# Top-k attention with a dropless mixture of experts: tails of the transposed weights in the score banks

## The chip, the cores and the metric

One core of one Trainium2 chip. The metric is the device time of one launch in microseconds (us); 1531.04 us is the median of three runs of the kernel before (1531.03 to 1531.17). Engines: TensorE (PE, with its weight loads as PEld), VectorE (DVE), ScalarE (ACT), GpSimd (POOL), and SyncE (SP), which issues most transfers.

## The reference

```python
# q, k, v: (8, 8, 576, 64) float32
scores = (q @ k.T) / 8                          # per batch and head, 576 x 576
kth    = 32nd largest score of each row
attn   = softmax over the scores >= kth         # the rest weighs nothing
x      = (attn @ v) laid out as (4608, 512)
# experts: 8, w1 (512, 1024), w2 (1024, 512) each
logits = x @ w_gate
e      = argmax(logits);  gate = softmax(logits)[e]
y      = gate * (relu(x @ w1[e]) @ w2[e])       # each token in its own expert alone
```

## The kernel before

**Units and iterations.** A unit is one batch and two heads; there are 32, four to a batch. A unit's score rows are nine tiles of 128 rows (four per head, and one that holds the last 64 rows of both heads). They are worked in five groups: `groups` 0 to 3 are pairs (the same rows of both heads), group 4 is the single ninth tile. `loop()` runs over all 160 groups; one turn of it is an iteration.

**One iteration i**, in the order in which `loop()` writes it (inside `tc.manual_schedule`, so TensorE, ScalarE and VectorE keep exactly this order; GpSimd's elementwise steps are kept in order too):

1. VectorE: `fold` and `search`. `fold` takes maxima and minima of the two halves of a score row, `fold_on` halves the maxima once more and puts them into the tile `few` (L262), with the few largest of what was put aside. `search` finds the 32nd largest by four rounds of eight maxima (L307) and three replacements into `scr` (L314). `fold_on` of the next group is called inside this search, before its last round.
2. ScalarE: the small `low` (L323), then `depths`: one Relu per tile (L337), which marks scores below the threshold.
3. GpSimd: `less`, a subtraction per tile (L346), then `doubts` (L327), which reads `few`.
4. ScalarE: `scores(i + 3)`, copies of the score products of three iterations ahead from PSUM into `s` (L245).
5. `transposed(i - 1)`: TensorE turns the weights of the group before. Four 128x128 transposes per tile (L371) go into a bank `wTm` and are copied by ScalarE into `wT` (L374, L376). The last 64 columns of each tile, the tails (L380), go into a bank `wTl` of their own and are copied into `wTt` (L383, L385). `bank()` hands out the two banks of the pool `ps_t` in turn, for these and for everything else of attention.
6. ScalarE: `weights`, one Exp per tile (L357).
7. TensorE: `products(i + 4)`, the score products (L236) into PSUM tiles `sc` of two banks each, two tiles in the pool `ps_s`.
8. In certain iterations, steps of the unit's ending: in group 3, and again in the next unit's group 0, half of the outputs `po` (L401) with ScalarE's copy into `oT` (L403); in group 1 transposes back (`px`, `pl`) and the gate's logits, with copies (L418 to L420). Once a batch, ranks (L476 to L482) in group 4 and the copy of `run` (L800). `ending()` is a generator; `at_place()` moves it on at named places.

**Expert blocks.** A block is 128 tokens of one expert: `xtp` transposes, 32 products `ph` in eight pieces of four (each half of `ph` ends in a Relu copy `hT`, L651), eight pieces `py` (L661), and a scaled copy `y` (L675) that GpSimd then stores. `pieces(n)` runs the next n pieces of the current block on TensorE, and ends early where the block pauses (before `py`, so that `hT` can be made) or where the next block's rows aren't on chip yet; the rest goes back into `credit`. Copies that a piece makes due wait in the list `due` until `evacuate()` writes them into ScalarE's order. Pieces come in two calls per iteration: half of `now` between the transposes and the tails, the rest at the iteration's end. Expert rows are known once a batch has been routed, so pieces begin after about 400 us. After the last unit, the remaining blocks run alone.

**Buffers in play.** [...] `few` has two buffers, `scr` two, `s` four, `w` three.

Of the kernel before, what the change touches and what calls it, by code (L numbers as in the profile page):

```python
# [9 lines left out]
F32 = mybir.dt.float32  # L10
# [25 lines left out]
def kernel(  # L36
# [39 lines left out]
    nc = tc.nc  # L76
    B, U, P, _, S = qk.shape
# [3 lines left out]
    D = P // 2  # L81
# [119 lines left out]
    def bank(name):  # L201
        return k.ps_t.tile([P, SM], F32, name=name, tag="t")
# [23 lines left out]
    def products(n, tiles):  # L226
        todo = []
        got = []
        for i in tiles:
            ps = k.ps_s.tile([P, 2, SM], F32, name="sc")  # L230
            todo += [(ps, h, rows, cols) for h, rows, cols in parts(i)]
            got.append(ps)
        for j in range(2):
            for ps, h, rows, cols in todo:
                d = slice(h * D, (h + 1) * D)
                nc.tensor.matmul(  # L236
                    ps[rows, j, 0:HF], n.q[d, cols], n.k[d, j * HF:(j + 1) * HF], start=True, stop=True
                )
        return got

    def scores(got):

        s = k.att.tile([P, 2, 2, HF], F32, name="s", bufs=2 if k.exact else 4)
        return s, [
            lambda m=m, ps=ps: nc.scalar.copy(s[:, m, :, :], ps[:, :, 0:HF]) for m, ps in enumerate(got)  # L245
        ]

    def fold(tiles, s):

# [8 lines left out]
    def fold_on(tiles, f):  # L258

        m2 = slice(0, len(tiles))  # L260
        f.few = k.att.tile([P, 2, LW], F32, name="few")
        nc.vector.tensor_tensor(f.few[:, m2, 0:QF], f.h[:, m2, 0:QF], f.h[:, m2, QF:HF], op=ALU.max)  # L262
        f.hl = k.att.tile([P, 2, QF], F32, name="hl", bufs=1)
        nc.vector.tensor_tensor(f.hl[:, m2, :], f.h[:, m2, 0:QF], f.h[:, m2, QF:HF], op=ALU.min)
# [16 lines left out]
    def search(n, tiles, s, f, then=lambda: None):  # L281

        m_all = range(len(tiles))
        m2 = slice(0, len(tiles))
        tops = k.small.tile([P, 2, TOP_K], F32, name="tops", bufs=4)
        if k.exact:
            src = [s[:, m, :, :].rearrange("p j k -> p (j k)") for m in m_all]
            width = S
        else:
            src = [f.few[:, m, :] for m in m_all]  # L290
            width = LW
            for m in m_all:
                for j, away in enumerate((f.l[:, m, :], f.hl[:, m, 0:QF // 2], f.hl[:, m, QF // 2:QF])):
                    nc.vector.max(out=f.few[:, m, QF + 8 * j:QF + 8 * j + 8], in_=away)  # L294
        scr = k.att.tile([P, 2, width], F32, name="scr")
        nbias = k.small.tile([P, 2], F32, name="nbias", bufs=3)
        R = TOP_K // 8

        def quiet(r):

            return r >= (1 if len(tiles) == 2 else 2)

        for r in range(R):
            if r == R - 1:
                then()
            for m in m_all:
                nc.vector.max(out=tops[:, m, r * 8:(r + 1) * 8], in_=src[m])  # L307
# [15 lines left out]
        nc.scalar.activation(low[:, m2], thr[:, m2], AF.Copy, scale=STEEP)  # L323

        def doubts():
            c = 2 * tiles[0] if len(tiles) == 2 else 2 * NC
            k.last_pool = in_turn(nc.gpsimd.tensor_tensor(  # L327
                n.over[:, c:c + len(tiles), :], f.few[:, m2, QF + 7:LW:8], _inner(thr[:, m2], NL), op=ALU.subtract
            )).ins

        return low, nbias, doubts
# [27 lines left out]
                    accum_out=n.z[:, c + m:c + m + 1],  # L359
                )  # L360

    def transposed(n, tiles, w):

        pair = len(tiles) == 2
        if tiles[0] == 0:
            n.wT = k.wtp.tile([P, NC, 2, S], F32, name="wT")
            n.wTt = k.wtp.tile([ST, 2, S], F32, name="wTt")
        for m, i in enumerate(tiles):
            pm = bank("wTm")
            for c in range(NC):  # L370
                nc.tensor.transpose(pm[:, c * P:(c + 1) * P], w[:, m, c * P:(c + 1) * P], ident)  # L371
            pm4 = pm[:, :].rearrange("p (c q) -> p c q", c=NC)
            if pair:
                nc.scalar.copy(n.wT[:, :, m, tiles[0] * P:(tiles[0] + 1) * P], pm4)  # L374
            else:
                nc.scalar.copy(n.wT[:, :, :, SM:S], pm4.rearrange("p c (h q) -> p c h q", h=2))  # L376
        yield
        pt = bank("wTl")
        for m in range(len(tiles)):
            nc.tensor.transpose(pt[0:ST, m * P:(m + 1) * P], w[:, m, SM:S], ident)  # L380
        if pair:
            q = slice(tiles[0] * P, (tiles[0] + 1) * P)
            nc.scalar.copy(n.wTt[:, :, q], pt[0:ST, 0:2 * P].rearrange("p (h q) -> p h q", h=2))  # L383
        else:
            nc.scalar.copy(n.wTt[:, :, SM:S], pt[0:ST, 0:P].rearrange("p (h q) -> p h q", h=2))  # L385

    def outputs(n, x):

# [303 lines left out]
    with ExitStack() as st:  # L692
# [147 lines left out]

        got_of, s_of, f_of, w_of = {}, {}, {}, {}

        def turning(i):
            b, u, g = work[i]
            return transposed(unit[b * U + u], g, w_of.pop(i))

        def multiply(i):
            b, u, g = work[i]
            got_of[i] = products(unit[b * U + u], g)
            if g == groups[-1] and b * U + u + 2 < len(units):  # L850
                unit.append(load_unit(*units[b * U + u + 2]))

        def loop():
            nonlocal credit, rate, clock
            for i in range(min(AHEAD, len(work))):
                multiply(i)
                s_of[i], steps = scores(got_of.pop(i))
                for step in steps:
                    step()
            multiply(AHEAD)  # L860
            f_of[0] = fold(work[0][2], s_of[0])
            fold_on(work[0][2], f_of[0])
            for i, (b, u, g) in enumerate(work):
# [28 lines left out]
                credit -= now  # L892
                clock = i
                if i + AHEAD < len(work):
                    s_of[i + AHEAD], steps = scores(got_of.pop(i + AHEAD))
# [20 lines left out]
            for _ in turning(len(work) - 1):  # L916
                pass
            assert len(late) == 1
            clock = None
            for count, _ in enumerate(late[0][0]):  # L920
# [24 lines left out]
    with ExitStack() as outer:  # L945
# [10 lines left out]
        with ExitStack() as st:  # L956
# [7 lines left out]
            with tc.For_i(0, B, 1) as b:  # L964
# [3 lines left out]
                for u in range(U):  # L968
# [1 line left out]
                    load_values(n)  # L970
                    open_unit(n)
                    for g in groups:
                        s, steps = scores(products(n, g))
# [6 lines left out]
                        for _ in transposed(n, g, w):  # L980
                            pass
                    for _ in outputs(n, x):
                        pass
                    for _ in divisors(n):
# [67 lines left out]
```

## Time and profile before

| | |
|---|---|
| median of three runs | 1531.04 us |
| the profiled execution | 1531.07 us, its span 1529.5 us |
| TensorE busy | 1334.9 us (87%), granted clock 0.91 on average |
| VectorE busy | 1134.8 us (74%) |
| ScalarE busy | 944.1 us (62%) |
| GpSimd busy | 646.5 us (42%) |
| DMA, mean | 151 GB/s |

By stages: from 0 to 400 us TensorE is busy 295.5, VectorE 371.2, ScalarE 276.5 us; from 400 to 1235 us 786.8, 756.2 and 622.6 us; from 1235 us on TensorE 252.6 of 294 us, and VectorE next to nothing.

In the rows of the profile `L371` is line 371 of the kernel; `wTm<-ident,w` says that an instruction writes `wTm` from `ident` and `w`. A time in brackets behind a row is how long its engine had stood idle, and who ended it. A matmul of this kernel is recorded twice, so a pair's eight transposes and its eight records of four score products are what their rows count.

### The profile page before, as it was taken

The page shows a single profiled execution, that of the slowest core. Times are in us where ns is not written, and L with a number is a line of the kernel's source. Part 1 is how long each engine was busy: PE and PEld are TensorE (multiplying, and loading weights), DVE is VectorE, ACT ScalarE, POOL GpSimd, SP SyncE. Part 2 cuts the span into 40 slices and gives each one's busy share as a digit, 9 for nine tenths or more (in the row PEclk, how much of TensorE's full clock was granted, in tenths as well). Part 3 has the DMA queues.
Part 4 walks back from the last instruction along what each step waited for, and adds up shares of the span by engine and source line. Part 5 has one row for each costly group of instructions (what it writes and reads, how often), then busy time and mean ns, then how long its engine had stood idle before and what let it go on. Part 6 is the DMA issues. An engine that isn't in the chain of part 4 may idle for free. (4 is left out here: it accounts for less than half of the span.)

```text
span 1529.5 us, 25597 instructions
## 1 busy us (share of the span) xinstructions
PE 1334.9 (87%) x8034; PEld 889.8 (58%) x8034; DVE 1134.8 (74%) x4702; ACT 944.1 (62%) x2097; POOL 646.5 (42%) x837
## 2 busy tenths in 40 slices
PE   5777777788799989998999999989999994999996
PEld 3444444445466656666666666657666672677673
DVE  7999989998999999999789989997899820000000
ACT  4777767765777778786776777777767640111110
POOL 3445456444644555464444644554436431000000
PEclk9877868765899999999999999999999996999998
DMA  2000011001534363526444444454444458688883
GB/s 71 25 25 25 25 38 43 25 25 37 197 135 168 126 219 129 183 96 244 171 158 163 173 149 151 154 175 176 170 173 173 164 182 270 248 293 317 302 305 133
DMA packets 101937, 230.70 MB, mean 151 GB/s; under 512 B 5150, under 2 KB 25630, under 8 KB 101792
## 3 DMA queue, kind: packets, MB, share of 16 engines
q1 hardware_dynamic: 95328, 209.00, 38.6%
q0 software_dynamic: 6464, 19.97, 3.6%
q8 instruction: 66, 1.08, 0.3%
q14 instruction: 79, 0.65, 0.1%
HBM read 207.68 MB, written 22.33 MB: 150 GB/s over the span
## 5 line engine op out<-in xcount | busy, mean ns | idle before, releaser
L346 POOL TENSOR_TENSOR w<-s,w 128x576 f32<-128x576 f32 x288 | 402.7, 1417 | 588.6 <-ACT w L337 588.5
L646 PEld LDWEIGHTS ph<-xTs,w 128*128 128x128 f32 x2560 | 301.2, 193 | 29.3 <-issue 29.3
L646 PE MATMUL ph<-xTs,w 128*128 128x128 f32 x2560 | 317.5, 279 | 0.0
L661 PE MATMUL py<-w,hT 128*128 128x512 f32 x640 | 296.8, 607 | 1.8 <-ACT hT L651 1.8
L236 PE MATMUL sc<-qkb 64*128 64x288 f32 (+1 forms) x1280 | 237.8, 495 | 23.9 <-ACT s L245 17.1
L307 DVE MAX8 tops<-scr 128x8 f32<-128x168 f32 x864 | 253.7, 323 | 2.3
L357 ACT ACTIVATE w<-w,nbias 128x576 f32<-128x576 f32 x288 | 221.4, 771 | 0.9 <-POOL w L346 0.9
L337 ACT ACTIVATE w<-s,low 128x576 f32<-128x576 f32 x288 | 209.5, 769 | 5.2
L661 PEld LDWEIGHTS py<-w,hT 128*128 128x128 f32 x640 | 117.2, 193 | 122.9 <-issue 118.1
L371 PE MATMUL wTm<-ident,w 128*128 128x128 f32 x1152 | 180.1, 300 | 9.2 <-ACT x L419 8.1
L371 PEld LDWEIGHTS wTm<-ident,w 128*128 128x128 f32 x1152 | 143.2, 153 | 62.5 <-issue 26.4
L314 DVE MATCH_REPLACE8 scr<-tops,scr 128x168 f32<-128x168 f32 x576 | 179.3, 317 | 0.0
L236 PEld LDWEIGHTS sc<-qkb 64*128 64x128 f32 (+1 forms) x1280 | 121.4, 203 | 92.0 <-issue 33.2
L245 ACT COPY s<-sc 128x576 f32<-128x576 f32 x288 | 168.3, 628 | 9.7 <-PE sc L236 9.7
L380 PE MATMUL wTl<-ident,w 128*64 128x128 f32 x288 | 65.7, 304 | 113.6 <-ACT wT L374 112.8
L401 PE MATMUL po<-wT,vb 128*64 128x288 f32 x1024 | 162.3, 467 | 0.6 <-ACT wT L376 0.6
L374 ACT COPY wT<-wTm 128x512 f32<-128x512 f32 x256 | 138.2, 597 | 26.2 <-PE wTm L371 26.0
L667 POOL DMA_INDIRECT out_dram<-y,xg x40 | 44.2, 1106 | 230.8 <-ACT y L675 226.8
L262 DVE TENSOR_TENSOR few<-h 128x288 f32<-128x288 f32 (+1 forms) x160 | 75.0, 469 | 75.7 <-POOL doubt L327 75.1
L294 DVE MAX8 few<-l 128x8 f32<-128x288 f32 x288 | 129.0, 448 | 0.0
L401 PEld LDWEIGHTS po<-wT,vb 128*64 128x64 f32 x1024 | 77.3, 157 | 84.1 <-issue 36.9
L253 DVE TENSOR_TENSOR h<-s 128x576 f32<-128x576 f32 (+1 forms) x160 | 116.2, 726 | 5.6 <-ACT s L245 5.6
(125 smaller groups left out, 1478.4 us busy)
## 6 DMA issues: line engine op xcount, KB each, us to landing
w<-in_moe_w_dram SPq DMA_DIRECT2D x80, 2048.0 KB, 12.8
qkb<-in_qk_dram SPq DMA_DIRECT2D x32, 576.0 KB, 4.1
xg<-x_rows SPq DMA_DIRECT2D x40, 257.0 KB, 2.7
vb<-in_v_dram SPq DMA_DIRECT2D x32, 320.0 KB, 3.2
x_rows<-blank SPq DMA_DIRECT2D x5, 257.0 KB, 10.0
x_rows<-blank POOLq DMA_DIRECT2D x4, 257.0 KB, 8.1
x_rows<-x,posi POOLq DMA_INDIRECT x40, 3.3
out_dram<-y,xg POOLq DMA_INDIRECT x40, 3.3
```

What stands on the lines that cost most here:

```text
L236: nc.tensor.matmul(ps[rows, j, 0:HF], n.q[d, cols], n.k[d, j * HF:(j + 1) * HF], start=True, stop=True)
L245: lambda m=m, ps=ps: nc.scalar.copy(s[:, m, :, :], ps[:, :, 0:HF]) for m, ps in enumerate(got)
L307: nc.vector.max(out=tops[:, m, r * 8:(r + 1) * 8], in_=src[m])
L314: nc.vector.match_replace(out=scr[:, m, :], in_to_replace=tops[:, m, r * 8:(r + 1) * 8], in_values=src[m], imm_value=NEG,)
L337: nc.scalar.activation(w[:, m, :], s[:, m, :, :].rearrange("p j k -> p (j k)"), AF.Relu, scale=-STEEP, bias=low[:, m:m + 1],)
L346: k.last_pool = in_turn(nc.gpsimd.tensor_tensor(w[:, m, :], s[:, m, :, :].rearrange("p j k -> p (j k)"), w[:, m, :], op=ALU.subtract)).ins
L357: nc.scalar.activation(w[:, m, :], w[:, m, :], AF.Exp, scale=scale, bias=nbias[:, m:m + 1], accum_out=n.z[:, c + m:c + m + 1],)
L371: nc.tensor.transpose(pm[:, c * P:(c + 1) * P], w[:, m, c * P:(c + 1) * P], ident)
L374: nc.scalar.copy(n.wT[:, :, m, tiles[0] * P:(tiles[0] + 1) * P], pm4)
L401: nc.tensor.matmul(po[r, 0:HF], lhsT, rhs, start=(c == 0), stop=(c == KC - 1))
L646: nc.tensor.matmul(ph[:, f, :], n.w1[:, 0, dt, fc * P:(fc + 1) * P], n.xT[:, dt, :], start=(dt == 0), stop=(dt == DT - 1),)
L661: nc.tensor.matmul(py, hT[:, f, :], n.w2[:, 0, f, :], start=(f == 0), stop=(f == FT - 1))
```

## The change

The score banks become one tile of four banks, `score_room()`, one buffer for a whole group. A score row uses 288 of the 512 columns of each bank; the transposed tails go into columns 288 to 415 of the same tile. So the iteration takes its room first, the tails are turned into it right behind the other transposes, and the score products of that iteration go into it afterwards. All copies of the turn then follow on ScalarE in one stretch: both of `wT`, then one of `wTt`.

`few` gets three buffers, `scr` one. `evacuate()` moves from behind the Relu marks to behind the score copies. In iterations with outputs, back transposes or ranks, and in every group 3, all pieces come behind those (`first` is 0); elsewhere the first half comes between tails and products. A block that starts no longer writes all due copies, only those up to `xT`.

```diff
-        for name, bufs in (("ps_s", 2), ("ps_t", 2), ("ps_m", 2)):
+        for name, bufs in (("ps_s", 1), ("ps_t", 2), ("ps_m", 2)):
...
+    def score_room():
+        return k.ps_s.tile([P, 2, 2, SM], F32, name="sc")
+
+    def products(n, tiles, ps):
         for j in range(2):
+            for m, i in enumerate(tiles):
+                for h, rows, cols in parts(i):
+                    d = slice(h * D, (h + 1) * D)
+                    nc.tensor.matmul(
+                        ps[rows, m, j, 0:HF], n.q[d, cols], n.k[d, j * HF:(j + 1) * HF], start=True, stop=True
+                    )
+        return ps
...
-        f.few = k.att.tile([P, 2, LW], F32, name="few")
+        f.few = k.att.tile([P, 2, LW], F32, name="few", bufs=3)
...
-        scr = k.att.tile([P, 2, width], F32, name="scr")
+        scr = k.att.tile([P, 2, width], F32, name="scr", bufs=1)
...
-    def transposed(n, tiles, w):
+    def transposed(n, tiles, w, ps):
...
+        pm = [bank("wTm") for _ in tiles]
+        for m in range(len(tiles)):
             for c in range(NC):
+                nc.tensor.transpose(pm[m][:, c * P:(c + 1) * P], w[:, m, c * P:(c + 1) * P], ident)
+        pt = ps[0:ST, 0:len(tiles), 0, HF:HF + P]
+        for m in range(len(tiles)):
+            nc.tensor.transpose(pt[:, m, :], w[:, m, SM:S], ident)
+        q = slice(tiles[0] * P, (tiles[0] + 1) * P) if pair else slice(SM, S)
+        for m in range(len(tiles)):
+            pm4 = pm[m][:, :].rearrange("p (c q) -> p c q", c=NC)
             if pair:
+                nc.scalar.copy(n.wT[:, :, m, q], pm4)
             else:
+                nc.scalar.copy(n.wT[:, :, :, q], pm4.rearrange("p c (h q) -> p c h q", h=2))
-        yield
-        pt = bank("wTl")
...
+        nc.scalar.copy(n.wTt[:, :, q], pt if pair else pt[:, 0, :].rearrange("p (h q) -> p h q", h=2))
...
     def block(n, following=lambda: None, put_off=lambda store: store()):
...
-        evacuate()
+        evacuate("xT")
...
                 w_of[i] = depths(g, s_of[i], low)
-                evacuate()
                 less(g, s_of.pop(i), w_of[i])
...
                     for step in steps:
                         step()
+                evacuate()
                 at_place("turn")
+                room_for = score_room()
                 if i:
-                    turns = turning(i - 1)
-                    next(turns)
-                rest = pieces(now - now // 2)
-                if i:
-                    next(turns, None)
+                    turning(i - 1, room_for)
+                first = 0 if any(end[1] == "products" for end in late) or g == groups[-2] else now - now // 2
+                rest = pieces(first)
                 weights(n, g, w_of[i], nbias)
                 evacuate()
                 if i + AHEAD + 1 < len(work):
-                    multiply(i + AHEAD + 1)
+                    multiply(i + AHEAD + 1, room_for)
                 if g == groups[-2]:
                     end = ending(b, u)
                     late.append([end, next(end)])
                 at_place("products")
                 at_place("weights")
-                credit = min(credit + pieces(now // 2 + rest), 6 * rate)
+                credit = min(credit + pieces(now - first + rest), 6 * rate)
```

More of the change, by code (lines that the diff above doesn't have):

```diff
@@ L224, in parts, with scores @@
         return [(h, slice(h * ST, (h + 1) * ST), slice(SM, S)) for h in range(2)]
[L226 to L232, printed above, removed]
-        for j in range(2):
[L234 to L241, printed above, removed]
+    def score_room():
+        return k.ps_s.tile([P, 2, 2, SM], F32, name="sc")
+    def products(n, tiles, ps):
+        for j in range(2):
+            for m, i in enumerate(tiles):
[5 more added lines that the diff above has]
+        return ps
+    def scores(tiles, ps):
         s = k.att.tile([P, 2, 2, HF], F32, name="s", bufs=2 if k.exact else 4)
-        return s, [
-            lambda m=m, ps=ps: nc.scalar.copy(s[:, m, :, :], ps[:, :, 0:HF]) for m, ps in enumerate(got)
-        ]
+        return s, [lambda m=m: nc.scalar.copy(s[:, m, :, :], ps[:, m, :, 0:HF]) for m in range(len(tiles))]
     def fold(tiles, s):
@@ L367, in transposed @@
             n.wTt = k.wtp.tile([ST, 2, S], F32, name="wTt")
-        for m, i in enumerate(tiles):
-            pm = bank("wTm")
+        pm = [bank("wTm") for _ in tiles]
+        for m in range(len(tiles)):
             for c in range(NC):
-                nc.tensor.transpose(pm[:, c * P:(c + 1) * P], w[:, m, c * P:(c + 1) * P], ident)
-            pm4 = pm[:, :].rearrange("p (c q) -> p c q", c=NC)
+                nc.tensor.transpose(pm[m][:, c * P:(c + 1) * P], w[:, m, c * P:(c + 1) * P], ident)
[5 more added lines that the diff above has]
+            pm4 = pm[m][:, :].rearrange("p (c q) -> p c q", c=NC)
             if pair:
-                nc.scalar.copy(n.wT[:, :, m, tiles[0] * P:(tiles[0] + 1) * P], pm4)
+                nc.scalar.copy(n.wT[:, :, m, q], pm4)
             else:
-                nc.scalar.copy(n.wT[:, :, :, SM:S], pm4.rearrange("p c (h q) -> p c h q", h=2))
-        yield
-        pt = bank("wTl")
[L379 to L385, printed above, removed]
+                nc.scalar.copy(n.wT[:, :, :, q], pm4.rearrange("p c (h q) -> p c h q", h=2))
+        nc.scalar.copy(n.wTt[:, :, q], pt if pair else pt[:, 0, :].rearrange("p (h q) -> p h q", h=2))
     def outputs(n, x):
@@ L841, with turning, multiply @@
         got_of, s_of, f_of, w_of = {}, {}, {}, {}
-        def turning(i):
+        def turning(i, ps):
             b, u, g = work[i]
-            return transposed(unit[b * U + u], g, w_of.pop(i))
-        def multiply(i):
+            transposed(unit[b * U + u], g, w_of.pop(i), ps)
+        def multiply(i, ps):
             b, u, g = work[i]
-            got_of[i] = products(unit[b * U + u], g)
+            got_of[i] = products(unit[b * U + u], g, ps)
             if g == groups[-1] and b * U + u + 2 < len(units):
@@ L855, in loop @@
             for i in range(min(AHEAD, len(work))):
-                multiply(i)
-                s_of[i], steps = scores(got_of.pop(i))
+                multiply(i, score_room())
+                s_of[i], steps = scores(work[i][2], got_of.pop(i))
                 for step in steps:
                     step()
-            multiply(AHEAD)
+            multiply(AHEAD, score_room())
             f_of[0] = fold(work[0][2], s_of[0])
@@ L894, in loop @@
                 if i + AHEAD < len(work):
-                    s_of[i + AHEAD], steps = scores(got_of.pop(i + AHEAD))
+                    s_of[i + AHEAD], steps = scores(work[i + AHEAD][2], got_of.pop(i + AHEAD))
                     for step in steps:
                         step()
+                evacuate()
                 at_place("turn")
+                room_for = score_room()
                 if i:
-                    turns = turning(i - 1)
-                    next(turns)
-                rest = pieces(now - now // 2)
-                if i:
-                    next(turns, None)
+                    turning(i - 1, room_for)
+                first = 0 if any(end[1] == "products" for end in late) or g == groups[-2] else now - now // 2
+                rest = pieces(first)
                 weights(n, g, w_of[i], nbias)
@@ L913, in loop @@
                 at_place("weights")
-                credit = min(credit + pieces(now // 2 + rest), 6 * rate)
-            for _ in turning(len(work) - 1):
-                pass
+                credit = min(credit + pieces(now - first + rest), 6 * rate)
+            turning(len(work) - 1, score_room())
             assert len(late) == 1
@@ L972 @@
                     for g in groups:
-                        s, steps = scores(products(n, g))
+                        s, steps = scores(g, products(n, g, score_room()))
                         for step in steps:
@@ L979 @@
                         weights(n, g, w, nbias)
-                        for _ in transposed(n, g, w):
-                            pass
+                        transposed(n, g, w, score_room())
                     for _ in outputs(n, x):
```

## The prediction, made before the changed kernel ran

> **What bounds the kernel now.** I read the page's 40 slices first, then who waited for whom in the stage where attention and expert blocks overlap, then the timeline of single iterations.
>
> ```profile
> PE   5777777788799989998999999989999994999996
> ...
> DVE  7999989998999999999789989997899820000000
> ...
> PEclk9877868765899999999999999999999996999998
> ```
>
> Three stages: to 400 us attention alone (VectorE full, TensorE at clock 0.76), to about 1235 both together, then expert blocks alone. The diff leaves the third stage's order as it was, so the first two decide.
>
> ```profile
> ACT oT L403 <- PE po L401: 79.6, 43, 3.2
> ...
> DVE few L262 <- POOL doubt L327: 62.1, 35, 5.3
> ACT wTt L383 <- PE wTl L380: 57.2, 43, 3.9
> ...
> PE wTl L380 <- ACT wT L374: 40.8, 28, 2.6
> ...
> ACT run L800 <- PE rank L482: 12.6, 5, 2.8
> ...
> ACT low L323 <- DVE tops L307: 8.0, 12, 0.8
> ```
>
> These are the waits from 400 to 1240 us (total, times, longest). VectorE looks full, but ScalarE hardly ever waits for its maxima (8.0 us); ScalarE waits for TensorE (79.6 and 57.2) and TensorE for ScalarE (40.8). The two are tied in a ring, each in its written order; VectorE's 62.1 us on `few` is the ring's lateness handed on through GpSimd. TensorE is idle only some 48 of 835 us there. So the length of that ring decides, above all in iterations without pieces to cover it.
>
> The ring's prices, start to next start, on ScalarE (low, relus, scores, weights, tails, Exp):
>
> ```profile
> 605.09 0.40 ACT L403 COPY oT<-po 128x288 f32<-128x288 f32 x1 [2.01 <-PE po L401]
> 605.39 0.21 ACT L323 ACTIVATE low<-tops 128x1 f32<-128x1 f32 x1
> 605.63 0.78 ACT L337 ACTIVATE w<-s,low 128x576 f32<-128x576 f32 x1
> 606.31 1.16 ACT L245 COPY s<-sc 128x576 f32<-128x576 f32 x2
> 607.36 1.08 ACT L374 COPY wT<-wTm 128x512 f32<-128x512 f32 x2
> 608.45 0.37 ACT L383 COPY wTt<-wTl 64x256 f32<-64x256 f32 x1
> 608.72 0.77 ACT L357 ACTIVATE w<-w,nbias 128x576 f32<-128x576 f32 x1
> ```
>
> oT 0.30, low 0.23, relu 0.68 a tile, scores 0.53 a tile, weights 0.54 a tile, tails 0.27, Exp 0.73 a tile; by the same reading hT 0.5, xT 0.55, y 0.6, logits with rows 0.95. On TensorE:
>
> ```profile
> 562.10 0.41 PE L380 MATMUL wTl<-ident,w 128*64 128x128 f32 x2 [2.60 <-ACT wT L374]
> 562.43 2.19 PE L236 MATMUL sc<-qkb 64*128 64x288 f32 x8
> 564.55 2.85 PE L401 MATMUL po<-wT,vb 128*64 128x288 f32 x16
> ...
> 600.74 0.41 PE L380 MATMUL wTl<-ident,w 128*64 128x128 f32 x2 [1.65 <-ACT wT L374]
> 601.08 1.24 PE L236 MATMUL sc<-qkb 64*128 64x288 f32 x8
> 602.25 2.16 PE L401 MATMUL po<-wT,vb 128*64 128x288 f32 x16
> ```
>
> Transposes of a pair 0.95, tails 0.34, score products 1.17, outputs 2.72, last transposes with logits 1.62; a piece of `ph` 0.95, of `py` 0.87. After the wait of 2.60 us the products took 2.12 and the outputs 3.42 instead: the clock had been halved. After 1.65 us it had not.
>
> **What the change does to the ring.** (1) Tails no longer take a third bank: the wait for the first weights copy (40.8 us from 400 on, 65.5 from 50 to 400) goes. (2) What is late next: tails go into the new score room, which needs both score copies read, 0.54 earlier than that weights copy. But the products that follow go into the same tile, and in the built order they wait for the copy of those tails. On ScalarE it stands behind two weights copies. From the end of the score copies, a pair's products start today after 0.54 + 0.1 + 0.34 = about 1.0; then after 1.08 + 0.27 + 0.1 = 1.45. For the single tile (group 4, turned in the next unit's group 0) today's tails find a free bank, and products start as soon as the first score copy is read, 0.4 before the last one's end; then 0.54 + 0.27 + 0.1 = 0.9 after it. Queued behind the waiting products are the outputs, whose copy holds ScalarE's next low and relus. Even where TensorE is the late one, each turn costs 0.67: after the last transpose ScalarE needs 0.1 + 0.54 + 0.27 + 0.1, TensorE has only 0.34 of tails. In the built order pieces stand between tails and products only in some iterations.
>
> [...]
>
> (3) Pieces. A call ends at a block's pause. Today an iteration has two calls; where all pieces go behind the outputs there is one, and what the pause cuts off becomes credit for group 2. In the built order of a common unit (units 11 to 13, 15 to 17, 23 to 25) pieces per group 1, 2, 3, 4, 0 go from 7, 3, 1, 3, 2 to 1, 13, 0, 0, 2. Group 4 has no cover left. Besides, `y` now stands on ScalarE in group 2 behind eight `py`.
>
> (4) Three `few` rows: VectorE's waits are the ring's (above), so I give 5 us. One `scr`, written and read by VectorE alone in order: nothing; if VectorE became the bound, still nothing. (5) Relus and xT behind the score copies: 0.5 to 1.1 us later for them, earlier for the scores; their readers are pieces, and in a common unit they stand after it in any case. No DMA and no GpSimd step changes its order.
>
> **A common unit, worked.** Time 0 is TensorE's first transpose in group 2, ScalarE reaching it at -0.5. Score copies end at 2.1, hT and xT at 3.2, weights 4.3. Tails 2.6; seven `py` to 8.9, products 10.1, the eighth 10.95, five `ph` to 15.8. ScalarE takes `y` at 11.75, group 3's relus and scores to 14.4, hT to 15.5. Group 3: transposes 16.75, tails copied 17.8, products 19.05, outputs 21.8, oT 22.2. Group 4: scores 24.1, tails copied 25.5, products 26.7 (TensorE idle about 2.4). Group 0: scores 28.85, tails copied 29.7, products 30.9 (idle 2.4), outputs 33.6, two pieces. Group 1: scores 36.15, tails copied 37.5, products 38.8, logits 40.4, rows copied 41.35, a piece and xT to 41.85. That is the unit's period. From 22.8 to 29.8 TensorE works 2.1 of 7 us, so by the row at 562 I add cold products and outputs in group 0, 1.7: 43.5. The same working gives today's order 35.8; the timeline has 35.5 to 37.2, mean 36.0, in the six without ranks.
>
> **The sum.** Six common units at +7.5: 45. Three with ranks (today 39.0): ScalarE's copy of `run` waits for the ranks at 29.1, which makes 44.9, with half a cold stretch 45.4: +6.4 each, 19. Units 14, 18, 22, 26, 30, whose next block is late: pieces stay spread; the loss of 0.7 to 1.0 in four turns stands against the 2.6 us wait and its cold stretch; 39.5 worked, today 39.6 to 41.7: 0. The six with more pieces (19 to 21, 27 to 29): three uncovered turns at 0.67 each against about 1.2 of waits today, +2 each: 12. Units 1 to 10, without pieces: group 3 +0.3, group 0 +1.2, group 1 +0.4 makes 1.9 each, 19, less 5 for `few`: 14. Ends: +1. Together +91. The profiled execution took 1531.07 us (span 1529.5), within 0.03 of the median of the runs: 1622.
>
> Ends for the doubtful terms: first stage 0 (hidden by VectorE) to 20; common units 41.9 (never cold) to 45; late-block units -2 to +2; heavy units 0 to +3.
>
> [...]
>
> **Rivals.** *Drought absorbed*: the burst in group 2 lets ScalarE get ahead, so group 4 and 0 need no cover, and only the 0.67 to 1.0 per turn is paid: common units +1.9 (17), heavy 12, first stage 14: 1574. For it: ScalarE is busy only 623 of 835 us. Against it: `y` and then oT hold it just there. *Faster*: the removed wait frees TensorE and the third row frees VectorE, at most 40.8 + 12.9 = 54 us, of which half, 1504. It decides if ScalarE copies tails before TensorE comes to the products in nearly every turn, a lead of 1 us; against it the 57.2 us that ScalarE waits for TensorE and the order of the pieces. *Cold throughout*: the overlapped stage falls to the first stage's clock of 0.76 for a third of its units, some +8 us in seven of them beyond the sum: 1678.
>
> **Numbers.** Forecast 0.60, drought absorbed 0.20, faster 0.10, cold throughout 0.08, no change 0.02. The range of 1555 to 1660 takes in the forecast's ends and the absorbed drought. Within 0.2% (3 us) this kernel's measurement can tell nothing: faster 0.10, same 0.02, slower 0.88.
>
> **What would show it.** Right: waits of the score products on the tails' copy, of tails on the score copies in groups 4 and 0, a granted clock below 0.95 between 430 and 700 us, common units of 42 to 45 us, `few` waits nearly gone. Wrong: units of 36 us with TensorE idle under 2 us each, or ScalarE waiting for `tops` instead.

## The result and the profile after

| | before | after |
|---|---|---|
| median of four runs | 1531.03 us (1528.19 to 1531.17) | 1653.5 us (1636.25 to 1654.97) |
| the profiled execution | 1531.07 us, span 1529.5 | 1653.49 us, span 1651.9 |
| mean granted clock of TensorE | 0.91 | 0.887 |

The changed kernel is slower: ratio 1.0779, 95% interval 1.0707 to 1.0851. The page's busy and clock rows after the change, 40 slices of 41.3 us each:

```profile
PE   5777777777888889888898998888989896799996
...
DVE  7999999999987998889988998899899941000000
...
PEclk9877666667799889978999999999999999899998
```

The last copy of attention's outputs (`oT`) now ends at 1364.8 us instead of 1245.6, and what follows, mostly expert blocks alone, takes 287.1 us, where it took 283.9. Most of TensorE's nines of the overlapped stage have become eights. The clock is 0.72 to 400 us (0.76 before) and 0.94 from 400 to 1360 us (0.98 from 400 to 1235 before).

The waits of that stage, 400 to 1360 us (total, times, longest):

```profile
ACT oT L396 <- PE po L394: 136.6, 45, 5.1
...
DVE h L249 <- ACT s L242: 77.9, 39, 6.3
...
ACT y L668 <- PE py L654: 64.3, 14, 5.4
PE sc L234 <- ACT wTt L378: 59.2, 77, 1.8
PE sc L370 <- ACT s L242: 54.6, 46, 2.4
...
ACT run L793 <- PE rank L475: 23.7, 5, 6.8
```

The wait of the tails for the weights copy is gone, as the change meant. In its place stand two on the shared tile: tails (L370) wait for the score copies 54.6 us, and score products (L234) for the copy of the tails 59.2 us; both are listed for TensorE, which had waited 40.8 us. What hangs on TensorE is later too: `oT` 136.6 us instead of 79.6, and `y` 64.3 instead of 6.7. VectorE's wait on `few` is gone, but VectorE waits 77.9 us for ScalarE's scores instead of 62.1 for GpSimd.

To compare units, counted from 0 to 31, I cut both traces at the start of each unit's `low` of group 0 (sums in us):

| units | before | after | more | predicted |
|---|---|---|---|---|
| 1 to 10, without pieces | 370.2 | 390.2 | 20.0 | 14 |
| common: 11, 13, 15, 17, 23, 25 | 216.2 | 261.8 | 45.6 | 45 |
| with ranks: 12, 16, 24 | 117.1 | 147.3 | 30.2 | 19 |
| next block late: 14, 18, 22, 26, 30 | 202.8 | 199.0 | -3.8 | 0 |
| more pieces: 19 to 21, 27 to 29 | 242.7 | 262.9 | 20.2 | 12 |
| what lies before and after these | | | 10.2 | 1 |

The sum is 122.4, the difference of the two profiled executions. Where the cut lies matters a little: what hangs on a unit's group 4 partly falls behind the next unit's first `low`. Cut at TensorE's first transpose of group 1 instead, the common units take 44.7 us more, those with ranks 30.4, late blocks 2.9 less, and those with more pieces 18.8 more, so these two cuts read alike. In a common unit TensorE goes through the end of group 3 and groups 4 and 0 like this (unit 15):

```profile
661.15 1.23 PE L367 MATMUL wTm<-ident,w 128*128 128x128 f32 x8
663.70 0.41 PE L370 MATMUL sc<-ident,w 128*64 128x128 f32 x2 [1.32 <-ACT s L242]
664.91 1.24 PE L234 MATMUL sc<-qkb 64*128 64x288 f32 x8 [0.81 <-ACT wTt L378]
...
668.32 0.42 PE L370 MATMUL sc<-ident,w 128*64 128x128 f32 x1 [1.22 <-ACT s L242]
669.08 2.18 PE L234 MATMUL sc<-qkb 64*64 64x288 f32 x8 [0.35 <-ACT wTt L378]
671.20 3.06 PE L394 MATMUL po<-wT,vb 128*64 128x288 f32 x16
```

Each turn shows both new waits: tails 1.32 and 1.22 us behind score copies, products 0.81 and 0.35 behind the tails' copy. Nothing else stands there, so TensorE works only 3.0 of the 6.7 us from 662.4 to 669.1, and in group 0 the products take 2.18 instead of 1.24 us and the outputs 3.06 instead of 2.16: the granted clock was halved from 666.24 to 673.06. ScalarE in the same unit:

```profile
643.68 0.38 ACT L378 COPY wTt<-sc 64x256 f32<-64x256 f32 x1
...
650.97 0.69 ACT L668 ACTIVATE y<-py,xg 128x512 f32<-128x512 f32 x1 [5.38 <-PE py L654]
...
674.94 0.40 ACT L396 COPY oT<-po 128x288 f32<-128x288 f32 x1 [4.38 <-PE po L394]
```

`y` holds it 5.38 us in group 2, behind the eight `py`, and `oT` 4.38 us behind the cold outputs; the next low and Relus stand behind both.

### The profile page after: what moved, and what is told of

The parts are those of the page before. It is cut to its first block, busy times and chain, and to the rows that moved or that the text cites. A ratio compares the mean times of both kernels' runs of the same rounds, so it can differ in the third digit from the quotient of the medians.

```text
span 1651.9 us, 25693 instructions
## 1 busy us (share of the span) xinstructions
PE 1380.5 (84%) x8034; PEld 910.8 (55%) x8034; DVE 1230.0 (74%) x4702; ACT 933.1 (56%) x2097; POOL 696.7 (42%) x837
## 5 line engine op out<-in xcount | busy, mean ns | idle before, releaser
L342 POOL TENSOR_TENSOR w<-s,w 128x576 f32<-128x576 f32 x288 | 409.0, 1438 | 652.6 <-ACT w L333 652.4
L234 PE MATMUL sc<-qkb 64*128 64x288 f32 (+1 forms) x1280 | 249.4, 518 | 103.8 <-ACT wTt L378 90.1
L639 PEld LDWEIGHTS ph<-xTs,w 128*128 128x128 f32 x2560 | 295.6, 192 | 31.9 <-issue 28.0
L639 PE MATMUL ph<-xTs,w 128*128 128x128 f32 x2560 | 306.4, 277 | 1.5 <-DMA w<-in_moe_w_dram 1.0
L234 PEld LDWEIGHTS sc<-qkb 64*128 64x128 f32 (+1 forms) x1280 | 123.5, 210 | 188.0 <-ACT wTt L378 127.7
L249 DVE TENSOR_TENSOR h<-s 128x576 f32<-128x576 f32 (+1 forms) x160 | 139.3, 871 | 85.1 <-ACT s L242 85.0
L367 PE MATMUL wTm<-ident,w 128*128 128x128 f32 x1152 | 184.8, 306 | 8.1 <-ACT x L412 8.1
L367 PEld LDWEIGHTS wTm<-ident,w 128*128 128x128 f32 x1152 | 147.5, 157 | 52.8 <-issue 21.7
L394 PE MATMUL po<-wT,vb 128*64 128x288 f32 x1024 | 167.0, 476 | 0.6 <-ACT wT L377 0.6
L370 PE MATMUL sc<-ident,w 128*64 128x128 f32 x288 | 67.1, 309 | 107.6 <-ACT s L242 107.6
L396 ACT COPY oT<-po 128x288 f32<-128x288 f32 x64 | 25.5, 399 | 209.2 <-PE po L394 209.2
```

The source lines that it names most:

```text
L234: nc.tensor.matmul(ps[rows, m, j, 0:HF], n.q[d, cols], n.k[d, j * HF:(j + 1) * HF], start=True, stop=True)
L249: nc.vector.tensor_tensor(f.h[:, m2, :], s[:, m2, 0, :], s[:, m2, 1, :], op=ALU.max)
L342: k.last_pool = in_turn(nc.gpsimd.tensor_tensor(w[:, m, :], s[:, m, :, :].rearrange("p j k -> p (j k)"), w[:, m, :], op=ALU.subtract)).ins
L367: nc.tensor.transpose(pm[m][:, c * P:(c + 1) * P], w[:, m, c * P:(c + 1) * P], ident)
L394: nc.tensor.matmul(po[r, 0:HF], lhsT, rhs, start=(c == 0), stop=(c == KC - 1))
L639: nc.tensor.matmul(ph[:, f, :], n.w1[:, 0, dt, fc * P:(fc + 1) * P], n.xT[:, dt, :], start=(dt == 0), stop=(dt == DT - 1),)
```

## Experiments

Four kernels do one part of the change alone (one chip, kernel before 1525.93 us); three undo or move one part in the changed kernel (the kernel before 1525.77 us); four test the clock, one of them with VectorE's third row (1525.77 and 1522.15 us). Between executions with the same order of work the sum of units 1 to 10 differed by 5 us with before's order (365.4 to 370.9) and by 10 with the change's (380.9 to 390.9), so less than that is not read from one profile there.

**Sharing the score banks alone** (`a1_tails`). The new `transposed` and `score_room`, with `few`, `scr` and `evacuate()` as before and the pieces in two calls in every iteration, the first now between tails and products. Of its edit against the changed kernel, the line on the pieces:

```diff
-                first = 0 if any(end[1] == "products" for end in late) or g == groups[-2] else now - now // 2
+                first = now - now // 2
```

> The kernel before with the shared score room alone (tails turned right behind the other transposes into it, copies in one stretch, first half of the pieces now between tails and products); pieces, few, scr and evacuation as before. Ring theory: units 1 to 10, which have no pieces, lose the same 1.9 us each as in the full change (20 us by unit 11); in common units a piece covers the wait on the tails' copy, but the piece no longer covers the tails' wait for the scores, +1 to +2 us each. About 1580 us (1560 to 1600). Rival, that the pieces' order is nearly all of it: under 1545. Rival, that the sharing itself stalls ScalarE or TensorE in the bank: score products or copies longer by the row, above 1610.

Measured: 1576.83 us, ratio 1.0311 (1.0274 to 1.0347). Units 1 to 10 390.9 us, common 227.0, ranks 122.9, late blocks 189.3, more pieces 261.3. This part by itself makes all of the loss in the first stage (+20.7) and nearly all of that in the units with more pieces (+18.6). There the same loss stands at another wait: in units 19 to 21 the tails wait 10.2 us for the score copies and the products nothing, where in the changed kernel the products wait 9.0 us for the tails' copy and the tails 1.3. Where the next block is late it is a gain of 2.7 us a unit: the wait of 2.60 us on the weights copy is gone, behind which the clock was halved for 3.41 us in each of these units (562.58 to 566.00 us in unit 14).

**Pieces behind outputs alone** (`a2_pieces`), in the kernel before.

```diff
-                rest = pieces(now - now // 2)
+                first = 0 if any(end[1] == "products" for end in late) or g == groups[-2] else now - now // 2
+                rest = pieces(first)
...
-                credit = min(credit + pieces(now // 2 + rest), 6 * rate)
+                credit = min(credit + pieces(now - first + rest), 6 * rate)
```

> The kernel before with the new placing of pieces alone (all behind outputs, back transposes and ranks, one call). Pieces of a common unit go 7, 3, 1, 3, 2 to 1, 13, 0, 0, 2 in groups 1, 2, 3, 4, 0. Ring theory: units 1 to 10 exactly as before (37.0 mean); common units 40 to 42 us for 36.0, since group 4 and 0 have no cover, ranks +5; about 1595 us (1575 to 1615). Rival, that the drought is absorbed: common units within 1 us of before, under 1545.

Measured: 1599.39 us, ratio 1.0462 (1.0426 to 1.0498). Common units 243.5 us (+4.6 each), ranks 140.3 (+7.7 each), units 1 to 10 unchanged at 367.7. Its waits from 400 to 1290 us:

```profile
ACT oT L403 <- PE po L401: 102.3, 42, 4.2
...
PE wTl L380 <- ACT wT L374: 58.6, 54, 2.6
```

Without pieces ahead of the tails the old wait for the weights copy grows from 40.8 to 58.6 us, and the outputs come later (102.3 instead of 79.6). No bank is shared here: the order of the pieces costs this by itself. Both parts together cost a common unit 7.6 us where each alone costs 1.8 and 4.6; over the whole kernel the four parts alone sum to 51 + 73 + 7 + 7 = 138, the change to 122.

**Three `few` rows and one `scr` alone** (`a3_rows`), and **the new places of `evacuate()` alone** (`a4_evac`, with a starting block that writes only up to `xT`).

```diff
-        f.few = k.att.tile([P, 2, LW], F32, name="few")
+        f.few = k.att.tile([P, 2, LW], F32, name="few", bufs=3)
...
-        scr = k.att.tile([P, 2, width], F32, name="scr")
+        scr = k.att.tile([P, 2, width], F32, name="scr", bufs=1)
```

```diff
                 w_of[i] = depths(g, s_of[i], low)
-                evacuate()
...
                     for step in steps:
                         step()
+                evacuate()
                 at_place("turn")
```

> The kernel before with three rows of few and one of scr alone. Ring theory: VectorE's 75 us of waits on few vanish from that line and come back on the scores (h L253 from ScalarE) or as nothing; the time moves 0 to -8 us, 1527. Rival, that VectorE was the bound: -30 us or more, below 1500. Rival, that one scr costs: slower by some us with VectorE waits on scr.

> The kernel before with the copies of expert blocks behind the score copies, and a starting block that writes only up to xT, alone. Ring theory: order of four to five ScalarE copies per unit changes by about 1 us, mostly behind pieces: -4 to +4 us, 1531. Rival, that y behind eight py blocks ScalarE by itself: above 1545, with ScalarE waits of y on py of several us per unit.

Measured: 1533.2 us, ratio 1.0035 (1.0005 to 1.0066), and 1532.7 us, ratio 1.004 (0.9998 to 1.0081). Neither gains. The rows take VectorE's 75.1 us of waits on `few` away altogether and give nothing back for it; the groups of `a3_rows` on VectorE show where it went (form, count, busy us, mean ns, idle before):

```profile
L253 DVE TENSOR_TENSOR h<-s 128x576 f32<-128x576 f32 x128 | 111.9, 874 | 27.3 <-ACT s L245 27.1
...
L262 DVE TENSOR_TENSOR few<-h 128x288 f32<-128x288 f32 x128 | 77.0, 602 | 0.0
L264 DVE TENSOR_TENSOR hl<-h 128x288 f32<-128x288 f32 x128 | 70.6, 552 | 0.0
```

Before, the same three groups had means of 797, 449 and 451 ns. The steps got longer, and `h` waits 27.1 us for scores, where it waited 5.6.

**Two rows again, in the changed kernel** (`d_rows2`): the same lines, undone.

```diff
-        f.few = k.att.tile([P, 2, LW], F32, name="few", bufs=3)
+        f.few = k.att.tile([P, 2, LW], F32, name="few")
...
-        scr = k.att.tile([P, 2, width], F32, name="scr", bufs=1)
+        scr = k.att.tile([P, 2, width], F32, name="scr")
```

> The changed kernel with two rows of few and two of scr as before. Theory of the shared path: with three rows VectorE no longer waits for GpSimd, and its two-input steps run into GpSimd's subtractions instead; the h, l, few and hl steps took 377 us before and 456 after. With two rows they take about 380 again, VectorE's waits on few return (80 us or more), and the time stays within 10 us of the changed kernel, as VectorE is not the bound. Rival, that the third row gained time: slower by 10 us or more. Rival, that the longer VectorE steps cost time in units 1 to 10 (VectorE busy 382 of 400 us): faster by 10 us or more, nearly all there.

Measured: 1646.08 us, ratio to the kernel before 1.0772 (0.0007 below the change's own, within both intervals).

```profile
DVE few L258 <- POOL doubt L323: 163.2, 86, 6.2
```

VectorE now waits 163.2 us on `few`, and the time is what it was. So VectorE had room to wait, and the third row decides nothing here.

**A second call behind the pause** (`b2_two_calls`): the changed kernel, where a call of pieces that ends at a block's pause is followed by another, so that groups 3 and 4 get pieces again (7, 3, 1, 3, 2 in groups 1, 2, 3, 4, 0, as before the change; group 0 has its two in both).

```diff
-                credit = min(credit + pieces(now - first + rest), 6 * rate)
+                rest = pieces(now - first + rest)
+                if not first:
+                    rest = pieces(rest)
+                credit = min(credit + rest, 6 * rate)
```

> The changed kernel, but where all pieces come behind the outputs a second call follows a pause, so pieces of a common unit are 7, 3, 1, 3, 2 again in groups 1, 2, 3, 4, 0, all of group 1, 3 and 0 still behind the outputs. Ring theory: the burst of 13 in group 2 and the empty group 4 are what costs, not the place behind the outputs: common units back to 38.5 us from 43.6, units 1 to 10 unchanged (390 us); about 1595 us. Rival, that the place behind the outputs costs (nothing between tails and products in groups 1, 3, 0): common units stay above 42, 1635 or more.

Measured: 1599.35 us, ratio 1.0468 (1.0396 to 1.054). Common units 235.2 us, 39.2 each (43.6 in the change, 36.0 before); ranks 124.9. Its waits from 400 to 1290 us:

```profile
ACT oT L396 <- PE po L394: 116.0, 43, 5.6
...
PE sc L234 <- ACT wTt L378: 51.8, 70, 1.4
...
ACT y L668 <- PE py L654: 12.9, 7, 3.4
```

The burst in group 2 and the empty groups 3 and 4 are thus worth 26.6 of the 45.6 us in the common units and 22.4 of the 30.2 in those with ranks. `y` is back at 12.9 us, while the products still wait 51.8 on the tails' copy.

**The tails' copy one step earlier** (`b3_copy_order`): on ScalarE between the two copies of `wT` instead of behind both.

```diff
                 nc.scalar.copy(n.wT[:, :, :, q], pm4.rearrange("p c (h q) -> p c h q", h=2))
-        nc.scalar.copy(n.wTt[:, :, q], pt if pair else pt[:, 0, :].rearrange("p (h q) -> p h q", h=2))
+            if m == 0:
+                nc.scalar.copy(n.wTt[:, :, q], pt if pair else pt[:, 0, :].rearrange("p (h q) -> p h q", h=2))
```

> The changed kernel with the tails' copy between the two weights copies instead of behind both, so in pairs the score products may start 0.54 us earlier; nothing changes for the single tile. Ring theory: TensorE's 90 us of waits on the tails' copy fall by some 45, units 1 to 10 by 0.9 us each, common units by 1 us; about 1625 us (1610 to 1640). Rival, that this wait is hidden and only the pieces matter: no change, 1645 or more.

Measured: 1617.96 us, ratio 1.0616 (1.0531 to 1.0701). Over the whole span:

```profile
PE sc L370 <- ACT s L242: 123.8, 95, 2.9
...
PE sc L234 <- ACT wTt L379: 61.1, 125, 1.3
```

The products' wait falls from 90.1 us (the change, same view, also 125 times) to 61.1, while the tails' wait on the score copies rises from 107.6 to 123.8. The units gain 39.5 us: 14.6 in units 1 to 10, 9.2 in those with more pieces, 6.4, 6.1 and 3.2 in the others. Of the 14.6 up to 10 can be spread; by the ratios to the kernel before the gain is 25 us, by the profiled executions 38. So one copy's place in ScalarE's order, 0.5 us a turn, makes a fifth to a third of the change's loss.

**Filling TensorE's waits, before the change** (`f1_fill_before`, `f3_fill_more`). The question is how much of the first stage and of the droughts is the clock alone. Products of 128x256, whose results the transposes overwrite, are put ahead of tile 0's transposes in iterations without pieces; in `f3` also in iterations that are due pieces while no block is under way.

```diff
             pm = bank("wTm")
+            for _ in range(fill if m == 0 else 0):
+                nc.tensor.matmul(pm[:, 0:2 * P], ident, w[:, 0, 0:2 * P], start=True, stop=True)
...
+    FILL = (3, 2, 4, 4, 2)
...
-                    turns = turning(i - 1)
+                    turns = turning(i - 1, 0 if now and current is not None else FILL[groups.index(g)])
```

In `f1` the condition is only `now`.

> The kernel before with idle-filling products of 128x256 ahead of the transposes in iterations without pieces (3, 2, 4, 4, 2 in groups 0 to 4; their results are overwritten by the transposes). Theory of the clock: in units 1 to 10 the granted clock goes from 0.76 to above 0.9, score products and outputs fall from 2.1 and 3.7 to 1.2 and 2.7 us, and these units from 37.0 to about 35.5 us each, where VectorE bounds them: 10 to 15 us faster. Rival, that the fill delays the transposes by as much as the clock gives back: within 5 us or slower.

> The kernel before with the filling products of f1_fill_before, and also wherever no block is under way, which adds group 3 of units 10, 14, 18, 22, 26 and 30, where a wait of 2.6 us on the weights copy halves the clock today. Theory of the clock: f1's 9 to 15 us, and 1.5 us in each of five late-block units: about 10 to 20 us under the kernel before. Rival, that these five lose by the fill what they win by the clock: as f1.

Measured: `f1` 1517.03 us, ratio 0.9936 (0.9896 to 0.9976); `f3` 1506.29 us, ratio 0.9886 (0.9843 to 0.9929). The clock rows of the pages of `f1`, then `f3`:

```profile
PEclk9999999999999999999999999999999996999998
```

```profile
PEclk9989998999999999999999999999999996999998
```

The clock to 400 us is 0.96 instead of 0.76 in `f1`, and units 1 to 10 take 353.3 us instead of 370.2. So even before the change this stage was not held by VectorE alone. `f3` adds 8.1 us in the five late-block units (202.7 to 194.6): it fills the wait of 2.6 us, behind which the products and outputs had run cold (before the change the clock is halved for 3.41 us in each of the five; in unit 14 the products took 2.19 us, and in `f3` they take 1.24, behind a wait of 1.15). It is faster than both kernels of this case.

**The same filling in the changed kernel** (`f2_fill_after`): every group up to unit 10, then groups 4 and 0.

```diff
+        for _ in range(fill):
+            nc.tensor.matmul(pm[0][:, 0:2 * P], ident, w[:, 0, 0:2 * P], start=True, stop=True)
...
-                    turning(i - 1, room_for)
+                    turning(i - 1, room_for, FILL[groups.index(g)] if not left or g in (groups[0], groups[-1]) else 0)
```

> The changed kernel with the same idle-filling products: in all groups up to unit 10, and after that in groups 4 and 0 alone (2 and 3 of 128x256). Theory of the clock: the long waits of groups 4 and 0 halve the clock, which adds cold products and outputs; kept warm, units 1 to 10 go from 39.0 to about 36.5 and common units from 43.6 to about 42, ranks from 49 to 46: some 40 us less, about 1610 us, and the rest of the loss stays. Rival, that the waits alone make the loss and the clock nothing: within 10 us of the changed kernel. Rival, that the clock is all of it: below 1570.

Measured: 1612.54 us, ratio 1.0601 (1.0541 to 1.0662).

```profile
PEclk9999999988999999999989999999989998899998
```

The total is as expected, its parts are not. Units 1 to 10 fall from 390.2 to 350.5 us, below `f1`'s 353.3: with the clock held (0.96 to 400 us in both), sharing the banks costs nothing that shows there. VectorE is then busy 386 (`f1`) and 388 (`f2`) of the first 400 us, so there is little left for a shorter ring to give. Ranks fall by 4.0 each in the mean. But the common units gain only 1.4 us in all: 1.7 each in 13, 17 and 25, whose stretch from group 0 to group 1 goes from 10.1 to 8.2 us, and a loss of 1.3 each in 11, 15 and 23, where the same stretch goes from 9.8 to 11.1; that the filling delays a TensorE that is late there is argued, not shown. Part of this is the cut: the cold stretch behind 11, 15 and 23 (half speed from 492.15, 666.24 and 1017.81 us in the change) falls into the units with ranks. The units with more pieces lose 12.7 us, 2.1 each: the filling takes 2.5 us in each of them, and TensorE's idle time falls by only 0.3 to 0.5 us a unit. So filling holds the clock (0.96 to 400 us, 0.98 from there to 1235), but does not stand in for the pieces: where it covers no wait, it is added time.

**Filling with three rows** (`f4_fill_rows`): `f3` with the lines of `a3_rows`, to see whether a warm TensorE makes VectorE the bound.

```diff
-        f.few = k.att.tile([P, 2, LW], F32, name="few")
+        f.few = k.att.tile([P, 2, LW], F32, name="few", bufs=3)
...
-        scr = k.att.tile([P, 2, width], F32, name="scr")
+        scr = k.att.tile([P, 2, width], F32, name="scr", bufs=1)
```

> f3 with three rows of few and one of scr. With a warm clock VectorE is near the bound in units 1 to 10 (34.4 us each, VectorE busy 386 of 400). Theory of the shared path: the third row takes away its waits on few but lets its two-input steps run into GpSimd's subtractions, h, l, few and hl some 30 to 80 us longer in all: 0 to 10 us slower than f3. Rival, that VectorE's waits were now the bound: 5 to 10 us faster than f3.

Measured: 1507.01 us, ratio 0.9886 (0.9845 to 0.9927): no difference from `f3`, so VectorE's waits on `few` are not the bound with a warm TensorE either (clock 0.92 to 400 us, 0.99 from there to 1235).

## Why the prediction was right, and where it was off

The direction, the mechanism and the range held; 1622 is 31 us short of the profiled execution, and four terms of the sum were too small: ranks by 11, more pieces by 8, the first stage by 6, and the ends by 9.

- **What is late next: right.** The wait for the weights copy is replaced by tails on score copies and products on the tails' copy. `a1_tails` shows the price of sharing alone, `b3_copy_order` that the products' place behind that copy is a large part of it.
- **The common unit: right, 45.6 us against 45 (44.7 by the other cut), and its working can be read off the trace.** Counted as in the working, from group 2's first transpose, five of the six take 43.0 to 43.8 us, where 43.5 was worked, and unit 25 takes 40.9. (They took 36.4 each before, so by this count the sum is +39.4; the change moves pieces from group 1 to group 2, so across this cut.) In unit 15 that transpose is at 639.59; from there, group 3's transposes start at 15.65 (worked: the five `ph` ahead of them end at 15.8), its products at 17.7 (copy worked at 17.8), outputs end at 21.6 (21.8), `oT` follows at once. Group 4's waits sum to 2.1 us and group 0's to 1.6; worked 2.4 each. The 1.7 us added for the cold group 0 is there: 0.94 more in the products and 0.90 in the outputs. Behind unit 25 the clock was not halved, so not every common unit pays it. `b2_two_calls` undoes the burst and gives back 4.4 of the 7.6 us.
- **Units with ranks: mis-sized, 30.2 instead of 19.** The term "half a cold stretch", 0.5 us a unit, was too small in two of the three. TensorE in unit 16, before the change and then in it:

```profile
646.30 1.04 PE L478 MATMUL rank<-oh,ones 128*128 128x32 f32 x8
...
647.41 1.26 PE L481 MATMUL rank<-oh,ones 128*128 128x8 f32 x10
```

```profile
708.40 2.29 PE L234 MATMUL sc<-qkb 64*128 64x288 f32 x8 [0.80 <-ACT wTt L378]
...
711.07 1.85 PE L471 MATMUL rank<-oh,ones 128*128 128x32 f32 x8
...
713.20 2.28 PE L474 MATMUL rank<-oh,ones 128*128 128x8 f32 x10
```

  Group 4 has the same two waits as in unit 15, 1.32 and 0.80 us, but here the clock is halved from 707.20 on, behind the first of them, one group earlier than I had it: products 2.29 instead of 1.24, and the rank products from 710.62 to 715.90, 5.3 us, where they took 2.85 before. That is 3.5 us of cold work, in unit 12 as well (5.3 us). In unit 24 the rank products kept the full clock (2.85 us). The three units lost 11.1, 11.5 and 7.7 us, and `f2_fill_after`, which fills group 4, brings all three to about 45 us.
- **Units 1 to 10: size about right, in part by luck, and the reason half wrong, 20.0 instead of 14.** In two more kernels with the change's order there it is 17 (`d_rows2`, 387.0) and 11 (`b2_two_calls`, 380.9), so 6 is within the spread. The 5 us that I took off for `few` don't exist (`a3_rows`: 370.9 against 370.2). And the loss is not the shifted products as such, from which the 19 was worked: with the clock held at 0.96 it vanishes (`f2_fill_after`, 350.5 against 353.3). In the change the clock is 0.72 to 400 us instead of 0.76, and a transpose of these units takes 356 ns in the mean instead of 335. My opening reading, "VectorE full", was wrong by the 17 us that `f1` gains there.
- **Units with more pieces: mis-sized, 20.2 instead of 12.** I took off 1.2 us a unit of today's waits and priced three turns at 0.67. In units 19 to 21 the products alone wait 9.0 us, 3.0 a unit, and TensorE's idle time rises from 4.1 to 12.3 us. `a1_tails` loses 18.6 us there by sharing alone, though at the tails' wait instead of the products', and the tails' copy moved up gives 9.2 back.
- **Late-block units: right,** -3.8 against 0; sharing by itself would be -13.5, the wait of 2.6 us and its 3.41 us of halved clock; the pieces' order alone changes nothing there (202.2), and why the two together give back most of the gain was not taken apart.
- **Ends: mis-sized, 10 instead of 1.** From unit 31's first `low` to its last `oT`, 49.4 us pass, where 43.1 us pass before the change and 43.1 and 43.2 in two kernels with before's order there (`a3_rows`, `f1`): these 6.3 us are the change's, and the sum gave unit 31 no term of its own. What lies behind that `oT` took 283.9 us before, 287.1 in the change, and 287.4 and 288.3 in those two kernels, so its 3 us need not be the change's.
- **The cold group 0, a doubtful term: right to count it.** It rested on one row, the wait of 2.60 us at 562; in the change shorter waits stood ahead of the fall: in unit 15 the clock was halved at 666.24, behind group 4's waits of 1.32 and 0.81 us and before group 0's began.
- **Rivals.** Drought absorbed (1574): refuted by `a2_pieces`, where the order of pieces by itself costs 27 us in the common units and 23 in those with ranks. Faster (1504): no part alone is faster. Cold throughout: from 400 to 1360 us the clock fell for 13 stretches of 3.4 to 20.5 us, mostly behind groups 4 and 0; the overlapped stage stands at 0.94, not 0.76.

## What to carry to other kernels

When a resource is freed by letting two users share another, look at who is copied out behind whom: the wait moves to the last reader of the shared tile, and the order of three short copies (0.5 us a turn) was worth 25 to 38 us. Price independent work by what it covers, not by when it is done: collected in one burst it left groups 3 and 4 bare, and spreading it again won 49 us in the common units and those with ranks, about what sharing alone cost (51 us). And here TensorE's clock was a second price on short waits close together: behind 1.32 and 0.81 us came 6.82 us at half speed. Work that is thrown away, put into such waits, made the kernel before the change 1.1% faster (0.7 to 1.6%).

## What the runs showed of the hardware beyond this

**VectorE's waits on GpSimd were worth nothing here: without them its steps ran beside GpSimd's and took longer.** With two `few` rows VectorE waits until GpSimd's subtractions and `doubt` are through. With three it starts earlier, beside those subtractions, and its two-input steps get longer: `few` of 128x288 from a mean of 449 to 626 ns in the changed kernel, single ones up to 1.6 us, and the two-input steps `h`, `l`, `few` and `hl` together from 376.9 to 455.3 us. Of the 128 `few` steps of that size, 51 overlap a GpSimd subtraction and take 903 ns in the mean, the other 77 take 443; with two rows none overlaps one before the change, and the mean is 449 there and 450 in `d_rows2`. The maxima over 288 columns (448 ns before, 444 in the change) and the replacements (317 and 314 ns) did not get longer. The 75.1 us of waits that the third row removes in `a3_rows` come back as longer steps (422.2 us, 45.3 more) and as 21.5 us more of waiting for scores.

**In these traces the same waits halved the clock or not, by where they fell.** In the traces before and after the change, 67 stretches of half speed end within the trace, and each lasts 1 to 7 whole steps of 3.41 us: from 562.58 to 566.00 before the change, and from 666.24 to 673.06 and 707.20 to 724.26 in it, for instance, one, two and five steps. In the step ahead of these three falls TensorE stood idle 2.60 us (one wait), 1.68 us (parts of two waits) and 1.32 us (one wait). The wait of 1.65 us at 600.74 lay across two steps, 1.04 and 0.61 us, and did not halve it. Counted in such steps over these two traces, all 22 full-speed steps that stood idle for 60% or more were followed by half speed, as were 26 of 27 between 50 and 60%, 15 of 55 between a third and a half, and 6 of 618 below a third; what caused these last was not looked into. None of the 73 half-speed steps with more than 20% idle was followed by full speed. Products thrown away held the clock of the first 400 us at 0.92 to 0.96 (`f1` to `f4`), where it had been 0.76 before the change and 0.72 in it.
